# Gated linear attention and a maxout FFN: the first part in another order, the decay check ahead of the last stores

## The chip, the cores and the metric

The kernel runs on one core of one Trainium2 chip. A core has five engines that each follow a program of their own: PE multiplies matrices, DVE (VectorE), ACT (ScalarE) and POOL (GpSimd) work on elements, and SP issues transfers. ACT issues some transfers too. The engines wait for each other through semaphores, and each engine runs its instructions in the order of its program. The metric is the time of one execution on the device in microseconds. The kernel before takes 504.13 us, the median of 3 runs (503.74 to 504.51).

## What is computed

The first stage is a recurrence with a decay per feature, for 4 batches, 8 heads, 768 tokens and 48 features per head. The second is a feed-forward block on its output, whose hidden layer is the largest of three products:

```python
f = 1.0 / (1.0 + np.exp(-f_logit))
for t in range(S):
    state = f[:, :, t, :, None] * state + np.einsum('bhd,bhe->bhde', k[:, :, t], v[:, :, t])
    y[:, :, t] = np.einsum('bhd,bhde->bhe', q[:, :, t], state)
x = y.transpose(0, 2, 1, 3).reshape(B * S, H * D)         # 3072 tokens of 384
h = np.maximum(np.maximum(x @ w1, x @ w2), x @ w3)        # 384 to 768, three times
return (h @ w_out).astype(np.float32)                     # 768 to 384
```

q, k, v and f_logit are 32-bit floats. The weights come as 64-bit floats, and the kernel rounds them itself to 32 bits with integer operations on the two words of each number.

## The kernel before

**Units and groups.** The recurrence is done in chunks of 64 tokens. One unit is a chunk of two batches, so there are 24 units; unit u uses the v tile u mod 4 and the state u mod 2. Four units make a group of 512 tokens, and the FFN runs once per group, six times in all.

**One unit.** `sigmoids(u)` makes the gates, `after(u)` scans them backwards and makes kh, `before(u)` scans them forwards and makes qh, `carry(u)` decays the state. `keys(u)` turns kh for the state update. `pairs(u)` multiplies kh and qh within the chunk (L319) and masks the result into `at` (L322). `values(u)` multiplies `at` by v (L333) and adds up the new state (L342, L350). `finish(u)` adds the product of qh and the carried state (L363), and ACT copies the sums to `heads` (L369). The first eight units are loaded by tokens (L158) and turned by PE (L234). From unit 8 on, `load(u)` of an even unit loads two units in blocks of 32 tokens with 24 transfers (L173), all of them on SP, and DVE turns the blocks (L238). Part of the blocks' padding is set by POOL (`pad_blocks`, L143).

**Packing.** `pack` moves a stretch of `heads` to `xT`, the FFN's input, with ten transfers (L380) for a whole group, or ten for the first three units on SP and five on SP with five on ACT for the fourth.

**The FFN.** `ffn(g, xT)` is a generator of 22 steps. The first 18 are products of one block of one input matrix with xT (L392); each writes a PSUM tile `p`, of which there are two. ACT copies the first of three to `top` (L396), DVE takes the maxima (L398). The last four steps, i = 0 to 3, are the output products of one unit's tokens (L411). ACT copies each to a tile `o` (L414), of which the pool holds two, and SP stores `o` with two transfers (L418). `fill(n)` runs n steps at the place where it is called, so the calls of `fill` in the main loop decide how FFN steps and units alternate in every engine's program.

**Rounding.** The weights are loaded in 24 pieces to 12 `raw` tiles. `round_begin(n)` has two ACT instructions (L211, L216), two on DVE (L212, L213) and one on POOL (L217); `round_end(n)` is one more on DVE (L225). Pieces 0 to 2 are rounded before the first FFN, the others during it: each of its 18 steps ends with `round_end(r)` and `round_begin(r + 1)`.

**Order.** It is written out by hand under `manual_schedule`: each engine's instructions stand in the order in which the Python code emits them. The tiles' waits are added by the framework, and so are those of the transfers: eight semaphores are used in turn, and each transfer waits until the one before it on the same semaphore has landed, whichever engine issued that one.

**The end.** The result is right only if no chunk decays too far. After the last FFN step, DVE takes the least decay of all (`ends`), a 1x1 product on PE (L542) counts the violations, and every engine reads the count `low` (L732) and branches past a slow general version (L733).

Of the kernel before, what the change touches and what calls it, by code (L numbers as in the profile page):

```python
# [9 lines left out]
FP32 = mybir.dt.float32  # L10
I32 = mybir.dt.int32
U32 = mybir.dt.uint32
AF = mybir.ActivationFunctionType
ALU = mybir.AluOpType
# [40 lines left out]
def kernel(  # L55
# [32 lines left out]
    def fast():  # L88
        ctx = ExitStack()
        with ctx:  # L90
# [47 lines left out]
                    nc.vector.memset(t[:, :, D:DP], pad)  # L138

            def pad_blocks(i):  # L140
                for nm, pad in PADS.items():
                    for p0 in (32, 96):
                        nc.gpsimd.memset(blocks[nm][i][p0:p0 + 32, :, :, D - 32:], pad)  # L143

            NLD = 4
            BY_ROWS = 8
# [31 lines left out]
            def load_v(u):  # L178
                load_tokens(v_tiles[u % NLD], v, u)
# [20 lines left out]

            halfway = {}

            def round_begin(n):
                if n in raw:
                    words = raw[n].rearrange("p (c two) -> p c two", two=2)
                    lo, hi = words[:, :, 0], words[:, :, 1]

                    top = work.tile([128, PIECE], U32, name="top_bits", bufs=4)  # L210
                    nc.scalar.activation(top.bitcast(FP32), hi.bitcast(FP32), AF.Abs)  # L211
                    nc.vector.tensor_scalar(top.bitcast(FP32), top.bitcast(FP32), HI_MIN, None, op0=ALU.max)  # L212
                    nc.vector.tensor_scalar(top, top, 3, 0x3FFFFFF8, op0=ALU.logical_shift_left, op1=ALU.bitwise_and)  # L213

                    rest = work.tile([128, PIECE], U32, name="rest_bits", bufs=3)
                    nc.scalar.activation(rest, lo, AF.Copy, scale=2.0 ** -29)  # L216
                    nc.gpsimd.tensor_tensor(top, top, rest, op=ALU.add)  # L217
                    halfway[n] = (top, hi)

            def round_end(n):  # L220
                if n in raw:
                    top, hi = halfway.pop(n)
                    dst = pieces[n][0].bitcast(U32)
                    by = lambda t: t.rearrange("p (a c) -> p a c", a=dst.shape[1])
                    nc.vector.scalar_tensor_tensor(dst, by(hi), 0xC0000000, by(top),  # L225
                                                   op0=ALU.bitwise_and, op1=ALU.bitwise_or)
                    raw.pop(n)
# [157 lines left out]
            def ffn(g, xT):  # L385
                hm = work.tile([128, NJ, TOK], FP32, name="hm", bufs=1)
                for j in range(NJ):
                    top = None
                    for i in range(3):
                        p = ps_f.tile([128, TOK], FP32, name="p")  # L390
                        for kt in range(NK):
                            nc.tensor.matmul(p, lhsT=w_in[i][:, kt, j * 128:(j + 1) * 128], rhs=xT[:, kt, :],  # L392
                                             start=(kt == 0), stop=(kt == NK - 1))
                        if i == 0:
                            top = work.tile([128, TOK], FP32, name="top")
                            nc.scalar.copy(top, p)  # L396
                        else:
                            nc.vector.tensor_tensor(hm[:, j, :] if i == 2 else top, p, top, op=ALU.max)  # L398

                        if g == 0:  # L400
                            step, last = 3 * j + i, 3 * NJ
                            for r in range(*(3 + (len(pieces) - 3) * n // last for n in (step, step + 1))):
                                round_end(r)
                                if r + 1 < len(pieces):
                                    round_begin(r + 1)
                            load_weights(2, r + 1)
                        yield
                for i in range(GRP):
                    p = ps_f.tile([128, TOK], FP32, name="p")
                    for j in range(NJ):  # L410
                        nc.tensor.matmul(p[:, 0:DM], lhsT=hm[:, j, i * UT:(i + 1) * UT], rhs=w_out[:, j, :],  # L411
                                         start=(j == 0), stop=(j == NJ - 1))
                    o = work.tile([UT, DM], FP32, name="o")
                    nc.scalar.copy(o, p[:, 0:DM])  # L414
                    c, bp = divmod(g * GRP + i, 2)
                    for a in range(2):
                        t0 = (2 * bp + a) * S + c * C
                        nc.sync.dma_start(out=out[t0:t0 + C, :], in_=o[a * C:(a + 1) * C, :])  # L418
                    yield
# [3 lines left out]
            def fill(n):  # L423
                while n and pending:
                    try:
                        next(pending[0])
                        n -= 1
                    except StopIteration:
                        pending.pop(0)

            def new_xT():
                return work.tile([128, NK, TOK], FP32, name="xT")

# [3 lines left out]
            with tc.manual_schedule():  # L437
# [2 lines left out]
                load(1, one, "kq")  # L440
                load_v(0)
                load(2)
                load_v(1)
                load(3)
                load_weights(3)
                load_v(2)
                load_v(3)
                xT = new_xT()
                sigmoids(0)
# [8 lines left out]
                for u in range(2):  # L458
                    values(u)
                    keys(u + 1)  # L460
                    after(u + 2)
                    carry(u + 2)
                    pairs(u + 1)
                    finish(u)
                    before(u + 2)
                    if u == 0:
                        sigmoids(3)
                values(2)
                keys(3)
                finish(2)  # L470
                load_weights(3)
                load(GRP)
                load_v(GRP)
                round_begin(0)
                pairs(3)
                round_begin(1)
                round_begin(2)
                values(3)
                for n in range(3):
                    round_end(n)  # L480
                round_begin(3)

                nc.tensor.transpose(ps_tr.tile([128, 128], FP32, name="tr"), ident, ident)
                finish(3)
                pack(0, GRP - 1, xT, both)
                load_weights(3)
                load(GRP + 1)
                load_v(GRP + 1)
# [7 lines left out]
                fill(1)  # L496
                for u in range(GRP, NU):
                    n = u + 1
                    fill(2 if u % 2 and u > 2 * GRP else 1)
                    keys(u)  # L500
                    if u > GRP:
                        finish(u - 1)
                        if u % GRP == 3:
                            pack(0, 2, xT)
                        elif u % GRP == 0:
                            pack(3, 3, xT, both)
                    if u % GRP == 0:
                        if u > GRP:
                            pending.append(ffn(u // GRP - 1, xT))
                        xT = new_xT()  # L510
                    pairs(u)
                    if u + 2 < NU and (u % 2 == 0 or u + 2 < BY_ROWS):
                        load(u + 2)
                    if u + 2 < NU:
                        load_v(u + 2)
                    if n < NU:
                        sigmoids(n)
                    fill(1)
                    if n < NU:
                        after(n)  # L520
                    fill(1)
                    values(u)
                    if n < NU:
                        before(n)
                        carry(n)
                        if n in (5, 7):
                            pad_blocks(n // 2 % 2)
                    fill(1)
                    if u >= 2 * GRP:
                        fill(1)  # L530
                fill(1)
                finish(NU - 1)
                pack(3, 3, xT, both)
                pending.append(ffn(NU // GRP - 1, xT))
                fill(99)


            least = work.tile([128, 1], FP32, name="least")
            nc.vector.tensor_reduce(out=least, in_=ends.rearrange("p u a -> p (u a)"), op=ALU.min, axis=AX.X)
            nc.vector.tensor_scalar(least, least, P_MIN, None, op0=ALU.is_lt)  # L540
            n_low = ps_tr.tile([1, 1], FP32, name="tr")
            nc.tensor.matmul(n_low, lhsT=least, rhs=ones, start=True, stop=True)  # L542
            nc.vector.tensor_copy(low, n_low)

    def general():
        G, AHEAD = 128, 3
# [218 lines left out]
```

## Time and profile before

| | |
|---|---|
| median of 3 runs | 504.13 us |
| the profiled execution's own time | 504.31 us |
| its span, first to last instruction | 502.6 us |
| PE busy | 467.9 us (93%) |
| DVE busy | 217.2 us (43%) |
| ACT, POOL busy | 108.7 us, 98.7 us |
| mean granted clock of PE | 0.966 |
| first full FFN stretch begins | 46.34 us |
| last output product ends | 495.14 us |

The profile comes from one execution. Its page gives the busy time of each engine, the span in 40 slices, the transfers, the chain of waits that ended last, and groups of instructions. Further answers of the trace are a timeline (start and duration in us, engine, line, operation, output and inputs, and in brackets how long the engine had been idle and what ended that), busy time in chosen stretches, and sums of waits. PEld is PE's loading of weights, which overlaps its products. A matmul of 32-bit floats stands in the trace as two instructions. SPq and ACTq are the transfers issued by SP and ACT: the time given there is that of issuing, not of moving the data.

### The profile page before, as it was taken

What the parts mean: (1) busy time and instruction counts of PE and PEld (TensorE: products, weight loads), DVE (VectorE), ACT (ScalarE), POOL (GpSimd) and SP (SyncE); (2) the same over time, 40 slices, a digit from 0 to 9 for tenths busy, and PEclk for the clock granted to TensorE, in tenths of its full rate; (3) what the DMA queues carried; (4) which work ended last, traced back from release to release, by engine and by line L of the source; (5) the groups of instructions that cost most, each with busy time, mean ns of one, the idle gap of its engine ahead of it and who ended that gap; (6) DMA issues with size and microseconds to landing.
All of it is one profiled execution on the core that took longest, in us unless ns stands there. A gap on an engine that the chain in (4) does not pass through costs nothing.

```text
span 502.6 us, 9969 instructions
## 1 busy us (share of the span) xinstructions
PE 467.9 (93%) x4067; PEld 250.9 (50%) x4067; DVE 217.2 (43%) x346; ACT 108.7 (22%) x227; POOL 98.7 (20%) x132
## 2 busy tenths in 40 slices
PE   5755999996989999999999999999999999999994
PEld 4642555543635455645545654545644545544452
DVE  7852787787225435135535226533325620012100
ACT  2340445540212211202220211220220111100000
POOL 2111356564021212021112022112112200000000
PEclk9875999998999999999999999999999999999998
DMA  9995996720156612266602276402460011200011
GB/s 129 199 179 157 268 243 143 93 59 1 40 87 109 88 27 65 46 79 110 85 2 63 56 88 109 66 16 57 78 105 18 1 36 37 55 0 0 1 28 42
DMA packets 170007, 38.51 MB, mean 77 GB/s; under 512 B 154976, under 2 KB 168800, under 8 KB 169952
## 3 DMA queue, kind: packets, MB, share of 16 engines
q1 hardware_dynamic: 166208, 36.50, 41.5%
q10 hardware_dynamic: 3744, 1.28, 1.3%
q8 instruction: 34, 0.56, 0.5%
q14 instruction: 21, 0.17, 0.1%
HBM read 28.31 MB, written 4.72 MB: 66 GB/s over the span
## 4 chain that ended last, share of the span: by engine, by line
PE 80%; DVE 6%; DMA 4%; SPq 4%; ACT 1%; issue 1%; POOL 1%; ACTq 0%; DVEq 0%; POOLq 0%
PE p L392 53%; PE p L411 17%; SPq L158 3%; PE y L363 2%; PE y L333 2%; DMA xT<-heads 2%; PE a L319 2%; PE tr L306 2%; PE y L342 1%; DMA v_ld<-in_v_dram 1%; POOL top_bits L217 1%; PE tr L234 1%; DVE top_bits L213 1%; DMA k_ld<-in_k_dram 1%; DVE top_bits L212 1%
## 5 line engine op out<-in xcount | busy, mean ns | idle before, releaser
L392 PE MATMUL p<-xT,w_in 128*128 128x512 f32 x648 | 291.9, 602 | 7.3 <-DMA xT<-heads 5.1
L392 PEld LDWEIGHTS p<-xT,w_in 128*128 128x128 f32 x648 | 120.5, 191 | 147.0 <-issue 134.1
L411 PE MATMUL p<-w_out,hm 128*128 128x384 f32 x288 | 98.8, 501 | 4.3 <-DVE w_out L225 4.3
L411 PEld LDWEIGHTS p<-w_out,hm 128*128 128x128 f32 x288 | 55.5, 195 | 44.7 <-DVE w_out L225 5.6
L398 DVE TENSOR_TENSOR top<-p,top 128x512 f32<-128x512 f32 x36 | 24.8, 690 | 106.3 <-PE p L392 106.3
L396 ACT COPY top<-p 128x512 f32<-128x512 f32 x36 | 21.1, 586 | 191.5 <-PE p L392 191.5
L279 POOL COPY ends<-r 128x8 f32<-128x8 f32 x24 | 4.6, 193 | 194.2 <-DVE r L273 194.2
L398 DVE TENSOR_TENSOR hm<-p,top 128x512 f32<-128x512 f32 x36 | 24.6, 684 | 38.2 <-PE p L392 38.2
L322 DVE TENSOR_TENSOR at<-a,mask 128x512 f32<-128x512 f32 x24 | 16.5, 689 | 52.8 <-PE a L319 52.8
L217 POOL TENSOR_TENSOR top_bits<-top_bits,rest_bits 128x384 uint32<-128x384 uint32 x24 | 27.2, 1133 | 50.3 <-DVE top_bits L213 27.9
L414 ACT COPY o<-p 128x384 f32<-128x384 f32 x24 | 11.4, 477 | 107.8 <-PE p L411 99.0
L287 DVE TENSOR_TENSOR_SCAN prod<-gate,from_inv 128x520 f32<-128x520 f32 x24 | 32.4, 1349 | 0.0
L273 DVE TENSOR_TENSOR_SCAN r<-gate,from_one 128x520 f32<-128x520 f32 x24 | 30.9, 1288 | 2.9 <-issue 2.2
L369 ACT COPY heads<-y 64x256 f32<-64x256 f32 (+1 forms) x72 | 26.6, 369 | 14.3 <-PE y L363 13.3
L291 POOL TENSOR_TENSOR qh<-qt,prod 128x512 f32<-128x512 f32 x16 | 18.8, 1178 | 41.7 <-DVE qt L238 41.7
L333 PEld LDWEIGHTS y<-at,v_ld 64*64 64x64 f32 x768 | 13.9, 136 | 20.9 <-issue 16.7
L333 PE MATMUL y<-at,v_ld 64*64 64x64 f32 x768 | 17.3, 227 | 5.7 <-ACT rest_bits L216 2.7
L308 ACT COPY ks<-tr 128x512 f32<-128x512 f32 x22 | 12.9, 586 | 41.2 <-PE tr L306 40.9
L280 POOL TENSOR_TENSOR kh<-kt,r 128x512 f32<-128x512 f32 x16 | 19.0, 1186 | 14.2 <-DVE kt L238 14.2
L297 POOL TENSOR_TENSOR state<-st,ends 128x384 f32<-128x384 f32 x22 | 21.1, 958 | 0.2
L238 DVE STREAM_TRANSPOSE gate<-sig 128x512 f32<-128x512 f32 x16 | 11.3, 708 | 21.2 <-ACT sig L254 21.2
L319 PE MATMUL a<-qh,kh 48*64 48x64 f32 x768 | 16.5, 225 | 0.5 <-DVE qh L291 0.5
(64 smaller groups left out, 269.9 us busy)
## 6 DMA issues: line engine op xcount, KB each, us to landing
raw<-in_moe_w_dram SPq DMA_DIRECT2D x18, 384.0 KB, 5.1
v_ld<-in_v_dram SPq DMA_DIRECT2D x48, 96.0 KB, 3.3
out_dram<-o SPq DMA_DIRECT2D x48, 96.0 KB, 2.2
raw<-in_moe_w_out_dram SPq DMA_DIRECT2D x6, 384.0 KB, 4.1
xT<-heads SPq DMA_DIRECT2D x30, 72.0 KB, 2.1
f_ld<-in_f_logit_dram SPq DMA_DIRECT2D x32, 64.0 KB, 2.9
k_ld<-in_k_dram SPq DMA_DIRECT2D x32, 64.0 KB, 2.8
q_ld<-in_q_dram SPq DMA_DIRECT2D x32, 64.0 KB, 2.8
```

The lines of the kernel that those rows point to most:

```text
L217: nc.gpsimd.tensor_tensor(top, top, rest, op=ALU.add)
L273: nc.vector.tensor_tensor_scan(r[:, 0:LEN][:, ::-1], flat(gate)[:, ::-1], flat(from_one)[:, ::-1], 1.0, op0=ALU.mult, op1=ALU.max)
L280: (nc.vector if u < BY_ROWS else nc.gpsimd).tensor_tensor(kh.rearrange("p h a t -> p a h t"), kt, by_batch(r[:, 1:LEN + 1].rearrange("p (x ...
L287: nc.vector.tensor_tensor_scan(flat(prod), flat(gate_tiles[u % 2]), flat(from_inv[u % 2]), 1.0, op0=ALU.mult, op1=ALU.max)
L297: nc.gpsimd.tensor_tensor(t, states[u % 2], ends[:, u, :].unsqueeze(2).to_broadcast([128, 2 * HP, D]), op=ALU.mult)
L319: nc.tensor.matmul(p[t, par, hp * C:(hp + 1) * C], lhsT=kh[r, hp, a, :], rhs=qh[r, a, hp, :], start=True, stop=True)
L333: nc.tensor.matmul(y[o:o + DP, a, hp * C:(hp + 1) * C], lhsT=v_ld[s, 2 * hp + par, :], rhs=d["at"][s, par, hp, :], start=(hp == 0), stop=F ...
L369: nc.scalar.copy(heads[o, :, t0 + a * C:t0 + (a + 1) * C], y[i, a, 0:HP * C].rearrange("p (h t) -> p h t", h=HP))
L392: nc.tensor.matmul(p, lhsT=w_in[i][:, kt, j * 128:(j + 1) * 128], rhs=xT[:, kt, :], start=(kt == 0), stop=(kt == NK - 1))
L396: nc.scalar.copy(top, p)
L398: nc.vector.tensor_tensor(hm[:, j, :] if i == 2 else top, p, top, op=ALU.max)
L411: nc.tensor.matmul(p[:, 0:DM], lhsT=hm[:, j, i * UT:(i + 1) * UT], rhs=w_out[:, j, :], start=(j == 0), stop=(j == NJ - 1))
```

## The change

1. In the first part SP's transfers are in another order: f of unit 3 ahead of v of unit 1, v of unit 2 ahead of the first three weight pieces, and q and v of unit 4 behind the first pack.
2. `round_begin` is split. Its ACT part stays, with a fourth `rest_bits` tile, and the DVE and POOL part becomes `round_middle`. The first two pieces are begun ahead of `values(2)`; five pieces are begun before the first FFN instead of four, and within it `round_end(r)` is followed by the beginning of piece r + 2.
3. `busy(n)` emits n products of constants of 256 columns into a `p` tile that nobody reads: one after `pairs(1)`, `pairs(2)` and `pairs(3)`, and 14 after the first pack.
4. `pad_blocks` is a generator, and each step of the first FFN takes one of its POOL instructions.
5. At the start of unit 8 no FFN step is run, where one was; all later steps of the FFN move back by one place.
6. The check of the decay is emitted eight steps after the last FFN is appended, and no longer after the last step.

```diff
             def pad_blocks(i):
+
                 for nm, pad in PADS.items():
                     for p0 in (32, 96):
-                        nc.gpsimd.memset(blocks[nm][i][p0:p0 + 32, :, :, D - 32:], pad)
+                        yield nc.gpsimd.memset(blocks[nm][i][p0:p0 + 32, :, :, D - 32:], pad)
...
             def round_begin(n):
                 if n in raw:
...
                     top = work.tile([128, PIECE], U32, name="top_bits", bufs=4)
                     nc.scalar.activation(top.bitcast(FP32), hi.bitcast(FP32), AF.Abs)
+
+                    rest = work.tile([128, PIECE], U32, name="rest_bits", bufs=4)
+                    nc.scalar.activation(rest, lo, AF.Copy, scale=2.0 ** -29)
+                    halfway[n] = (top, rest)
+
+            def round_middle(n):
+                if n in raw:
+                    top, rest = halfway[n]
...
                     nc.vector.tensor_scalar(top.bitcast(FP32), top.bitcast(FP32), HI_MIN, None, op0=ALU.max)
                     nc.vector.tensor_scalar(top, top, 3, 0x3FFFFFF8, op0=ALU.logical_shift_left, op1=ALU.bitwise_and)
-                    rest = work.tile([128, PIECE], U32, name="rest_bits", bufs=3)
-                    nc.scalar.activation(rest, lo, AF.Copy, scale=2.0 ** -29)
                     nc.gpsimd.tensor_tensor(top, top, rest, op=ALU.add)
...
                                 round_end(r)
-                                if r + 1 < len(pieces):
-                                    round_begin(r + 1)
+                                if r + 2 < len(pieces):
+                                    round_begin(r + 2)
+                                    round_middle(r + 2)
                             load_weights(2, r + 1)
+                            next(pads, None)
                         yield
...
+                    if g == 0:
+                        next(pads, None)
                     o = work.tile([UT, DM], FP32, name="o")
...
+            def busy(n):
+
+                p = ps_f.tile([128, TOK], FP32, name="p")
+                for _ in range(n):
+                    nc.tensor.matmul(p[:, 0:256], lhsT=ident, rhs=from_one.rearrange("p x t -> p (x t)")[:, 0:256],
+                                     start=True, stop=True)
+
+            pads = iter(())
...
                 load(2)
+                load(3, one, "f")
                 load_v(1)
-                load(3)
+                load(3, one, "kq")
+                load_v(2)
                 load_weights(3)
-                load_v(2)
                 load_v(3)
...
                     pairs(u + 1)
+                    busy(1)
                     finish(u)
...
+                for n in range(2):
+                    round_begin(n)
                 values(2)
+                for n in range(2):
+                    round_middle(n)
                 keys(3)
                 finish(2)
                 load_weights(3)
-                load(GRP)
-                load_v(GRP)
-                round_begin(0)
+                load(GRP, one, "fk")
                 pairs(3)
-                round_begin(1)
+                busy(1)
                 round_begin(2)
+                round_middle(2)
                 values(3)
-                for n in range(3):
-                    round_end(n)
-                round_begin(3)
+                round_end(0)
...
                 finish(3)
+                round_end(1)
+                round_end(2)
                 pack(0, GRP - 1, xT, both)
+                for n in range(3, 5):
+                    round_begin(n)
+                    round_middle(n)
+                busy(14)
+                load(GRP, one, "q")
+                load_v(GRP)
                 load_weights(3)
...
-                    fill(2 if u % 2 and u > 2 * GRP else 1)
+                    fill(0 if u == 2 * GRP else 2 if u % 2 and u > 2 * GRP else 1)
                     keys(u)
...
                 pending.append(ffn(NU // GRP - 1, xT))
+                fill(8)
+
+                least = work.tile([128, 1], FP32, name="least")
+                nc.vector.tensor_reduce(out=least, in_=ends.rearrange("p u a -> p (u a)"), op=ALU.min, axis=AX.X)
+                nc.vector.tensor_scalar(least, least, P_MIN, None, op0=ALU.is_lt)
+                n_low = ps_tr.tile([1, 1], FP32, name="tr")
+                nc.tensor.matmul(n_low, lhsT=least, rhs=ones, start=True, stop=True)
+                nc.vector.tensor_copy(low, n_low)
                 fill(99)
-
-
-            least = work.tile([128, 1], FP32, name="least")
...
```

More of the change, by code (lines that the diff above doesn't have):

```diff
@@ L201, in fast, with words @@
             halfway = {}
+            def words(n):
+                w = raw[n].rearrange("p (c two) -> p c two", two=2)
+                return w[:, :, 0], w[:, :, 1]
             def round_begin(n):
                 if n in raw:
-                    words = raw[n].rearrange("p (c two) -> p c two", two=2)
-                    lo, hi = words[:, :, 0], words[:, :, 1]
+                    lo, hi = words(n)
                     top = work.tile([128, PIECE], U32, name="top_bits", bufs=4)
                     nc.scalar.activation(top.bitcast(FP32), hi.bitcast(FP32), AF.Abs)
+                    rest = work.tile([128, PIECE], U32, name="rest_bits", bufs=4)
[4 more added lines that the diff above has]
+                    top, rest = halfway[n]
                     nc.vector.tensor_scalar(top.bitcast(FP32), top.bitcast(FP32), HI_MIN, None, op0=ALU.max)
                     nc.vector.tensor_scalar(top, top, 3, 0x3FFFFFF8, op0=ALU.logical_shift_left, op1=ALU.bitwise_and)
-                    rest = work.tile([128, PIECE], U32, name="rest_bits", bufs=3)
-                    nc.scalar.activation(rest, lo, AF.Copy, scale=2.0 ** -29)
                     nc.gpsimd.tensor_tensor(top, top, rest, op=ALU.add)
-                    halfway[n] = (top, hi)
             def round_end(n):
                 if n in raw:
-                    top, hi = halfway.pop(n)
+                    (top, _), (_, hi) = halfway.pop(n), words(n)
                     dst = pieces[n][0].bitcast(U32)
@@ L526, in fast @@
                         if n in (5, 7):
-                            pad_blocks(n // 2 % 2)
+                            pads = pad_blocks(n // 2 % 2)
                     fill(1)
@@ L534, in fast @@
                 pending.append(ffn(NU // GRP - 1, xT))
-                fill(99)
-            least = work.tile([128, 1], FP32, name="least")
[L539 to L543, printed above, removed]
+                fill(8)
[5 more added lines that the diff above has]
+                nc.vector.tensor_copy(low, n_low)
+                fill(99)
     def general():
```

## The prediction

> **What bounds the kernel now.** I read the page's summary first, then busy time by stretch.
>
> ```profile
> PE 467.9 (93%) x4067; PEld 250.9 (50%) x4067; DVE 217.2 (43%) x346; ACT 108.7 (22%) x227; POOL 98.7 (20%) x132
> ...
> PEclk9875999998999999999999999999999999999998
> ```
> ```profile
> 40.00:46.30 6.30, 2.05 (x2) 0.50 (x2) 1.21 (x4) 0.36 (x1) 0.99 (x1) 0.50 0.54 126
> 46.30:52.40 6.10, 6.06 (x13) 3.45 (x14) 0.98 (x3) 2.27 (x5) 0.30 (x1) 0.50 1.13 258
> ...
> 80.00:105.00 25.00, 24.70 (x266) 13.12 (x268) 21.89 (x41) 10.71 (x22) 12.94 (x13) 1.00 0.66 104
> 116.20:121.50 5.30, 0.96 (x4) 0.33 (x3) 3.89 (x9) 0.00 (x0) 2.37 (x3) 0.93 0.00 0
> 121.50:127.50 6.00, 6.00 (x10) 3.23 (x11) 2.13 (x3) 0.48 (x1) 1.96 (x2) 0.50 0.00 0
> ```
>
> In each stretch: PE, PEld, DVE, ACT, POOL, granted clock, DMA. From about 142 to 495 us PE never stops; it loses time only before. While x is packed (40 to 46.3) it is nearly idle, then runs 6.1 us at half clock. From 80 to 105 DVE, which rounds the weights, is 88% busy. At 116 to 121.5 PE waits for it, and 6 us at half clock follow. So the front is worth some 20 us, and any new PE stall after 142 is paid in full.
>
> The waits and the timeline at the first group boundary show one more thing:
>
> ```profile
> PE p L392 <- ACT o L414: 2.2, 1, 2.2
> ```
> ```profile
> 140.87 0.48 ACT L414 COPY o<-p 128x384 f32<-128x384 f32 x1 [0.59 <-DMA out_dram<-o]
> ...
> 141.95 1.10 PE L392 MATMUL p<-xT,w_in 128*128 128x512 f32 x2 [2.18 <-ACT o L414]
> ```
>
> An output copy waited for an earlier store to free one of two o tiles, and PE waited for the copy, because there are two p tiles. At the later boundaries this is free. SP at the second of them:
>
> ```profile
> 206.84 8.01 PE L411 MATMUL p<-w_out,hm 128*128 128x384 f32 x24
> ...
> 210.24 3.10 SPq L380 DMA_DIRECT2D xT<-heads  x5
> ...
> 213.39 5.27 SPq L173 DMA_DIRECT2D f_ld<-in_f_logit_dram  x8
> ...
> 223.00 4.15 SPq L173 DMA_DIRECT2D q_ld<-in_q_dram  x8
> ...
> 228.78 3.32 SPq L418 DMA_DIRECT2D out_dram<-o  x4
> ```
>
> Between the pack and the next stores SP issues 24 loads and two v loads: 213.4 to 228.7. The stores behind them are late, but nobody wants their tiles for 18 FFN steps.
>
> [...] SP sat 24.09 us on four xT issues at 110.99. [...] matmuls restarted at 46.34 and 121.47 and each ran about 6.1 us at 0.50. [...] here PE's branch took 4318 ns.
>
> **The change, part by part**, against the profiled span of 502.6 us.
>
> *Transfers by need, first part.* values(2) waited for v(2), which landed at 27.66 behind three 384 KB weight pieces. Issued before them it lands near 22.9 (those pieces land 1.1 us apart, and the last q of unit 3 at 21.93). f(3) goes ahead of v(1): PE's 2.3 us wait at 17.7 for f(3) shrinks by the two issues passed, 1.3 us. The mask product at(2), ready at 25.45 before, then sets values(2), at about 24. ACT's roundings of pieces 0 and 1 (landing 24.0 and 25.1) go ahead of keys(3), at 0.54 us each, four in all, so ks(3) is ready near 26.6. DVE does four roundings (4 x 0.36) before at(3). finish(3) then ends near 31 instead of 39.15. The pack doesn't gain all 8: its issues wait for semaphores of f(4) and k(4), and the DMA engines were solid until 36.2 (landing of k(4)); the last xT lands 40.0 instead of 46.3. **FFN start: -6.3** (-3 to -7.5). Moving q(4) and v(4) behind the pack costs nothing: q(4) lands near 41, and its transpose comes 6 us after the start.
>
> *Products of constants.* 14 matmuls of 256 columns: half of the 0.86 us that one 128x512 product takes at full clock, so 0.43 each, 6.0 us in all, 12.0 at half clock. They begin near 31 and end near 37 to 39, inside the pack's wait. At full clock from the start, the FFN saves half of 6.1 us. But the last one ends 1 to 3 us before xT[...]. **-2** (0 to -3.1). The three single ones stand where PE waits for DVE or ACT: nothing; without cover, 0.43 to 0.86 each.
>
> *Roundings two ahead.* DVE's finishing instruction waited for POOL 7.4 + 1.2 us between 60 and 130, and 2.1 more behind POOL's pad memsets (3.5 us in a lump at 105.7, now one per step). That is 10.7 us back on DVE, against a lag of 5.4 us (PE done at 111.87, hm at 117.27) plus about 3 us because PE now runs the stage faster. Enough: PE's waits at 116.22 (2.86) and 119.99 (1.48) and the half of 6 us at half clock go. **-7** (-2 to -7.7).
>
> *Decay check.* SP's read of the flag (0.73, 0.19 and 0.04 with gaps, 496.88 to 498.00) moves ahead of the last eight stores; SP's branch comes 1.1 us earlier[...]. [...] **-0.9** (-0.3 to -1.2). The check's one matmul is 0.2 us.
>
> *No FFN step at the start of unit 8.* This small edit shifts every later step by one, through all four boundaries (units 8, 12, 16, 20). Before: output tiles i=0 and i=1, keys/finish/pack/pairs, 24 loads, i=2 and i=3. After: i=0, pack, loads, then i=1, i=2, i=3. In SP's program two stores now stand ahead of the pack and six behind the loads. There are two o tiles: the copy of i=3 must wait for the store of i=1, and the second FFN step for that copy's p tile. With times from the start of i=0, taken from the later boundaries: i=0 to 3.9 (L411, 7.74 for two), keys to pairs 1.6, i=1 and i=2 to 13.4, values(12) 1.1, i=3 to 18.4, FFN step one (2.57) to 21.0; there PE stops. SP: the pack ends 5.2 after keys begin (352.67 to 357.88), at 9.1; from the first load to the second landed store 19.0, 18.5 and 18.3 in the three trace boundaries, so 27.6; the copy is done (0.48) at 28.2. PE idles 7.2 to 8.1, take 7.5. [...] **10.1 each, +30.3** for three (+26 to +36).
>
> Unit 8 is worse. In the order of the program the second to sixth DMA of the pack of units 4 to 6 now each wait for a DMA of ACT's own pack, which comes only after finish(7). Before, the ninth and tenth waited so (that was the 24.09 us). ACT's first xT lands 4.8 after keys begin (129.09 to 133.88), at 8.7; then nine xT (0.62 each), v(9) 1.4, the i=0 store 1.2 (to 16.9), the pack 3.1, loads 13.9, v(10) 1.5, the i=1 store 1.2 plus 2.2 to land: 38.8, copied at 39.5. xT is complete only at 22. PE idles 18.4 to 22, and 24.7 to 39.6: 18.6; with a clock loss of 2.6, and less the 2.6 of PE waits there before (138.2 to 141.95). **+18.7** (+12 to +22).
>
> Sum: 502.6 - 6.3 - 2 - 7 - 0.9 + 30.3 + 18.7 = 535.4. The profiled execution took 504.31 by the clock outside, the median is 504.13, so 1.5 lies around the span: **537 us**.
>
> **Rivals.** *A, as summed* (0.60): 530 to 544. *B, the front gives half* (0.20): if POOL or ACT stays late, PE still stalls at w_out[...]: 8 us less gain, 545. DVE's 88% speaks for it, the 10.7 us of waits against. *C, unit 8 is no worse than the others* (0.14): if the pack's semaphore order binds less than the program shows, that boundary costs 10.1 less 2.6 and not 18.7: 526. *D, the stores land in time* (0.05), the faster side: the loads between are 13.9 us of SP; under 6.4 us of them (21.0 less the pack's end 9.1, v 1.5, store 1.3, landing 2.2 and copy 0.5) PE would find its p tile free. Then 504.1 - 16.2 - 2.6 = 485. Against it: three boundaries of the trace have 13.8 to 15.3. That the edits cancel to nothing has 0.01.
>
> Faster or slower means by more than 0.2%, about what a measurement of this kernel can tell from no change: faster 0.05, same 0.01, slower 0.94. 80% range 524 to 548: all of A, most of B and C; D lies outside.
>
> **What would show it.** In the profile after: PE at L401 waiting for ACT's copy at L427 about 7 to 8 us three times and some 15 us once, ACT at L427 waiting for DMA out; half clock after each; out stores on SP after each 24 loads; FFN start near 40 at clock 1.00; no wait of L422 for w_out. Wrong if PE runs through the boundaries, or if the front gains under 8 us.

## The result, and the profile after

The changed kernel takes 535.54 us (median of four, 534.21 to 536.72) against 504.00 (503.74 to 504.51): 1.062 times as long, with a 95% interval of 1.060 to 1.065. The profiled execution took 535.54, its span 533.7. The forecast was 537 with a range of 524 to 548.

The page's summary and chain come first. Lines moved in the file by one to thirteen: L401 is the FFN product (L392 before), L422 the output product (L411), L427 the copy to `o` (L414), L431 the store of `o` (L418), L174 the later loads (L173).

```profile
PE 477.8 (90%) x4101; PEld 256.3 (48%) x4101; DVE 224.1 (42%) x346; ACT 109.0 (20%) x227; POOL 99.3 (19%) x132
...
PEclk9979999999599999889999969999979999999999
...
PE 68%; SPq 14%; DVE 7%; DMA 5%; issue 3%; ACT 1%; POOL 1%; ACTq 0%; DVEq 0%; POOLq 0%
PE p L401 49%; PE p L422 10%; SPq L174 9%; SPq L159 3%; PE y L372 2%; PE y L342 2%; DMA out_dram<-o 2%; SPq L389 2%; PE p L448 1%; PE a L328 1%; PE tr L315 1%; PE y L351 1%; DVE prod L296 1%; DMA raw<-in_moe_w_out_dram 1%; DMA v_ld<-in_v_dram 1%
```

PE now does 90% of a longer span. The clock keeps one early dip, in the third slice (half clock from 29.6 to 36.4 us). It has lost those from 40 us on, and has four new ones, one at each group boundary. SP's loads (`SPq L174`) hold 9% of the chain that sets the end.

The same stretches as before the change, in the view of busy time by stretch (PE, PEld, DVE, ACT, POOL, granted clock, DMA share, GB/s):

```profile
40.00:46.30 6.30, 6.30 (x25) 3.73 (x24) 2.65 (x6) 2.23 (x5) 2.04 (x3) 1.00 0.81 209
46.30:52.40 6.10, 6.10 (x19) 2.87 (x18) 5.93 (x10) 1.77 (x4) 2.50 (x4) 1.00 1.39 188
80.00:105.00 25.00, 25.00 (x320) 13.92 (x319) 23.73 (x41) 10.95 (x24) 13.88 (x16) 1.00 0.49 66
116.20:121.50 5.30, 5.30 (x78) 3.26 (x77) 2.03 (x5) 0.15 (x1) 1.37 (x2) 1.00 0.38 94
```

The first part does what it should. From 40 us PE is full and at full clock (up to 41 with the products of constants), DVE is 95% busy from 80 to 105 with PE never short of weights, and the idle 116 to 121.5 is gone. What comes after takes it back. The waits (us in total, times, longest) and the timeline, first at unit 8 and then at unit 12:

```profile
ACT o L427 <- DMA out_dram<-o: 67.6, 5, 18.3
...
PE p L401 <- ACT o L427: 36.7, 4, 15.3
...
SPq L389 <- DMA xT<-heads: 16.1, 1, 16.1
...
PE tr L574 <- DVE least L572: 1.3, 1, 1.3
```
```profile
112.70 6.29 SPq L389 DMA_DIRECT2D xT<-heads  x10
...
120.58 1.94 SPq L431 DMA_DIRECT2D out_dram<-o  x2
122.62 3.10 SPq L389 DMA_DIRECT2D xT<-heads  x5
125.76 4.31 SPq L174 DMA_DIRECT2D f_ld<-in_f_logit_dram  x8
...
134.36 4.20 SPq L174 DMA_DIRECT2D q_ld<-in_q_dram  x8
138.60 1.39 SPq L159 DMA_DIRECT2D v_ld<-in_v_dram  x2
140.09 4.54 SPq L431 DMA_DIRECT2D out_dram<-o  x6
...
143.02 0.48 ACT L427 COPY o<-p 128x384 f32<-128x384 f32 x1 [18.31 <-DMA out_dram<-o]
...
143.56 2.93 PE L401 MATMUL p<-xT,w_in 128*128 128x512 f32 x3 [15.30 <-ACT o L427]
...
227.08 1.22 PE L401 MATMUL p<-xT,w_in 128*128 128x512 f32 x1 [6.82 <-ACT o L427]
```

One pair of stores stands ahead of the last five transfers of the pack, and three pairs stand behind 24 loads. The copy of output tile 3 needs the tile that the store of tile 1 still holds, and so waits until 143.02. PE waits for that copy, 15.30 us here, 6.82 at unit 12, 7.20 and 7.40 at units 16 and 20.

### The profile page after: what moved, and what is told of

Its sections match the earlier page's. It is cut to its first block, busy times and chain, and to the rows that moved or that the text cites. A ratio compares the mean times of both kernels' runs of the same rounds, so it can differ in the third digit from the quotient of the medians.

```text
span 533.7 us, 10055 instructions
## 1 busy us (share of the span) xinstructions
PE 477.8 (90%) x4101; PEld 256.3 (48%) x4101; DVE 224.1 (42%) x346; ACT 109.0 (20%) x227; POOL 99.3 (19%) x132
## 4 chain that ended last, share of the span: by engine, by line
PE 68%; SPq 14%; DVE 7%; DMA 5%; issue 3%; ACT 1%; POOL 1%; ACTq 0%; DVEq 0%; POOLq 0%
PE p L401 49%; PE p L422 10%; SPq L174 9%; SPq L159 3%; PE y L372 2%; PE y L342 2%; DMA out_dram<-o 2%; SPq L389 2%; PE p L448 1%; PE a L328 1%; PE tr L315 1%; PE y L351 1%; DVE prod L296 1%; DMA raw<-in_moe_w_out_dram 1%; DMA v_ld<-in_v_dram 1%
## 5 line engine op out<-in xcount | busy, mean ns | idle before, releaser
L401 PE MATMUL p<-xT,w_in 128*128 128x512 f32 x648 | 298.7, 613 | 37.1 <-ACT o L427 36.7
L401 PEld LDWEIGHTS p<-xT,w_in 128*128 128x128 f32 x648 | 123.2, 196 | 182.3 <-issue 135.2
L422 PE MATMUL p<-w_out,hm 128*128 128x384 f32 x288 | 96.6, 490 | 0.5 <-DVE w_out L234 0.5
L407 DVE TENSOR_TENSOR top<-p,top 128x512 f32<-128x512 f32 x36 | 24.7, 687 | 165.5 <-PE p L401 165.3
L422 PEld LDWEIGHTS p<-w_out,hm 128*128 128x128 f32 x288 | 53.8, 190 | 38.1 <-issue 2.4
L427 ACT COPY o<-p 128x384 f32<-128x384 f32 x24 | 11.5, 477 | 151.0 <-PE p L422 80.1
L296 DVE TENSOR_TENSOR_SCAN prod<-gate,from_inv 128x520 f32<-128x520 f32 x24 | 35.0, 1459 | 0.0
L342 PEld LDWEIGHTS y<-at,v_ld 64*64 64x64 f32 x768 | 14.2, 137 | 16.8 <-issue 14.5
```

The lines of the kernel that those rows point to most:

```text
L296: nc.vector.tensor_tensor_scan(flat(prod), flat(gate_tiles[u % 2]), flat(from_inv[u % 2]), 1.0, op0=ALU.mult, op1=ALU.max)
L342: nc.tensor.matmul(y[o:o + DP, a, hp * C:(hp + 1) * C], lhsT=v_ld[s, 2 * hp + par, :], rhs=d["at"][s, par, hp, :], start=(hp == 0), stop=F ...
```

## The experiments

**Theory.** The one FFN step left out at the start of unit 8 makes all four stalls, through two `o` tiles and SP's order of issue, and the rest of the change is a gain. **Rivals:** the stalls come from the new first part, which leaves the queues later; the stores are late because transfers are slow or semaphores hold them, whatever the queue; PE would have waited at those places anyway.

A time below is the median of all executions. A ratio and its interval are of means that leave out the profiled execution, against the kernel before on the same chip: 504.26 us beside the first four versions, 503.81 beside the four that undo one part, 502.72 beside the other four. So a ratio is not just the quotient of two medians.

### The step put back, and the step alone

```diff
-fill(0 if u == 2 * GRP else 2 if u % 2 and u > 2 * GRP else 1)
+fill(2 if u % 2 and u > 2 * GRP else 1)
```

> The changed kernel with the FFN step at the start of unit 8 put back, all else kept. Theory (the shift of the steps by one makes all four stalls): the 36.7 us that PE waits for ACT's output copy go, and of the 19.1 us at half clock after the restarts (5.5, 3.9, 6.1, 3.6) half, 9.6; the small wait that the kernel before has at its first boundary (2 to 3) comes back: 535.5 - 36.7 - 9.6 + 2 = 491, range 486 to 494, below the kernel before by 10 to 18. Rival (the stalls come from the order of the first part, which leaves the queues later by the first boundary): the waits stay, 525 or more. Rival (PE would have waited there for something else anyway): 498 to 510.

Measured: 493.16 us (492.91 to 494.04), 0.9785 of before (0.9767 to 0.9803). The reverse edit in the kernel before:

```diff
-fill(2 if u % 2 and u > 2 * GRP else 1)
+fill(0 if u == 2 * GRP else 2 if u % 2 and u > 2 * GRP else 1)
```

> The kernel before with only the FFN step at the start of unit 8 left out. Theory: four stalls, three of 7.1 and one of about 15 us, and 9.6 for the clock, less the 2.6 that it waited there: 504 + 43 = 547, range 543 to 553. The prediction's own sum would give 504 + 49 = 553. Rival (the shift costs only with the new first part): 504 to 510.

Measured: 548.24 us (546.78 to 549.77), 1.0877 of before (1.0843 to 1.091). Its waits:

```profile
ACT o L414 <- DMA out_dram<-o: 64.9, 5, 19.0
...
PE p L392 <- ACT o L414: 34.8, 4, 14.2
```

Four waits, the longest 14.2 us, as in the changed kernel, with the old first part. The step costs 42.4 us on the new first part (535.54 - 493.16) and 44.0 on the old one (548.24 - 504.26). The first rival is out. With the step put back, one wait of another kind is left at unit 8:

```profile
PE p L401 <- DMA xT<-heads: 5.7, 1, 5.7
```

In the old order of steps PE has no output tiles left to do while `xT` of the second group is packed. The kernel before waited 2.2 us for an output copy at this place. So the third rival holds for 5.7 of the 36.7 us, and at one boundary alone.

### Three o tiles, and the stores on another queue

Both keep the step left out. The first has one more `o` tile, and three tiles instead of four for the scaled low words, to make room:

```diff
-o = work.tile([UT, DM], FP32, name="o")
+o = work.tile([UT, DM], FP32, name="o", bufs=3)
-rest = work.tile([128, PIECE], U32, name="rest_bits", bufs=4)
+rest = work.tile([128, PIECE], U32, name="rest_bits", bufs=3)
```

> The changed kernel, its shift kept, with three o tiles instead of two (and three tiles for the scaled low words instead of four, to make room). Theory (the copy of output tile 3 waits only because there are two o tiles and the store of tile 1 stands behind the loads): that copy now waits for the store of tile 0, issued ahead of the loads, so all four stalls go: 486 to 494 as with the step put back. Rival (the transfers themselves are too slow at the boundaries, or xT is late there): a stall of 3 to 7 us stays at each, 505 to 520.

Measured: 488.10 us (487.41 to 493.03), 0.9719 of before (0.9666 to 0.9773). Its page and timeline at unit 8:

```profile
PE 465.4 (96%) x4101; PEld 250.9 (52%) x4101; DVE 223.8 (46%) x346; ACT 109.5 (23%) x227; POOL 99.2 (20%) x132
...
PEclk9999999998999999999999999999999999999998
```
```profile
117.94 1.22 SPq L431 DMA_DIRECT2D out_dram<-o  x2
...
122.99 4.30 SPq L174 DMA_DIRECT2D f_ld<-in_f_logit_dram  x8
...
138.05 4.04 SPq L431 DMA_DIRECT2D out_dram<-o  x6
```

The six stores are as late as before, 20 us after the first two, and PE waits for none of them: tile 3 takes the `o` of tile 0, whose store went ahead of the loads. All four waits are gone. The 5.7 us for `xT` that the old order has at unit 8 are absent too, since the shifted order gives PE three output tiles to do meanwhile. The second leaves two `o` tiles and moves the stores to ACT's queue:

```diff
-nc.sync.dma_start(out=out[t0:t0 + C, :], in_=o[a * C:(a + 1) * C, :])
+nc.scalar.dma_start(out=out[t0:t0 + C, :], in_=o[a * C:(a + 1) * C, :])
```

> The changed kernel, its shift and its two o tiles kept, with all output stores issued from ACT's queue instead of SP's. Theory (the stores are late because they stand behind 24 loads in SP's program): they land 3 to 4 us after their copy, the three later stalls go; ACT pays about 1.2 us a pair of stores, which is 48 pairs x 1.2 less what is hidden, and ACT is idle three quarters of the time: 486 to 500. Rival (the stores are late because the DMA engines are full with the loads, or because their semaphores wait for loads): waits of 5 us or more stay at the boundaries, 515 to 540.

Measured: 492.23 us (491.45 to 493.81), 0.9763 of before (0.9744 to 0.9783). The timeline of ACT at unit 12:

```profile
199.76 1.16 ACTq L431 DMA_DIRECT2D out_dram<-o  x2
200.97 0.48 ACT L427 COPY o<-p 128x384 f32<-128x384 f32 x1 [1.23 <-PE p L422]
201.48 1.12 ACTq L431 DMA_DIRECT2D out_dram<-o  x2
205.30 0.48 ACT L427 COPY o<-p 128x384 f32<-128x384 f32 x1 [3.85 <-PE p L422]
```

The same stores beside the same loads land in time, and the third copy waits for PE alone. So the DMA engines were not too slow: the place in SP's program was it, and the second rival is out at the later boundaries. At unit 8 PE still waited 2.7 us, for `xT`.

### A smaller dose, and the shift one group later

The eight `q` loads of a pair of units go behind the stores of tiles 1 and 2 (step left out, two `o` tiles):

```diff
-load(u + 2)
+load(u + 2, one, "fk")
...
+if u + 2 < NU and (u % 2 == 0 or u + 2 < BY_ROWS):
+    load(u + 2, one, "q")
 values(u)
```

> The changed kernel (shift, two o tiles) with the eight q loads of each later pair of units issued behind the stores of output tiles 1 and 2 instead of ahead of them. Theory (what PE waits for is the time that SP spends on the loads ahead of the store): eight issues take 4.15 us, so the three later waits of 7.1 shrink to about 3.0 and leave no half clock behind, and the one at unit 8 of 15.3 to 11.1: 535.5 - 3 x (4.15 + 2.3) - 4.15 = 512, range 508 to 517. Rival (the store waits for the loads' semaphores or for busy DMA engines): 525 or more.

Measured: 516.81 us (514.79 to 518.44), 1.0278 of before (1.0245 to 1.031). The timeline of SP and PE at unit 12, then two stretches there:

```profile
208.49 4.15 SPq L174 DMA_DIRECT2D k_ld<-in_k_dram  x8
212.74 1.44 SPq L159 DMA_DIRECT2D v_ld<-in_v_dram  x2
214.27 2.51 SPq L431 DMA_DIRECT2D out_dram<-o  x4
216.87 4.30 SPq L174 DMA_DIRECT2D q_ld<-in_q_dram  x8
...
217.81 2.14 PE L401 MATMUL p<-xT,w_in 128*128 128x512 f32 x3 [2.66 <-ACT o L427]
```
```profile
215.20:218.60 3.40, 0.79 (x2) 0.49 (x3) 0.00 (x0) 0.97 (x2) 0.00 (x0) 1.00 0.72 155
218.60:222.00 3.40, 3.40 (x5) 1.35 (x4) 0.00 (x0) 0.00 (x0) 0.00 (x0) 0.51 0.69 87
```

Taking 4.15 us of issues away shortens the three later waits from 6.82, 7.20 and 7.40 to 2.66, 3.17 and 2.88: by 4.2 on average. That is the price of queue time one for one. (At unit 8 the wait fell further, from 15.30 to 8.73; why is open.) My total was 5 too low, because I had let the half clock go with waits so short. At unit 12 it stayed for 3.4 us (0.51 in the second stretch above), which is 1.7 lost; three times that is 5.1, an estimate from this one boundary. The further fall at unit 8 is offset in part in this trace by a first FFN product that comes 1.0 us later (42.01).

The last of this group leaves out the step at unit 12 instead of unit 8:

```diff
-fill(0 if u == 2 * GRP else 2 if u % 2 and u > 2 * GRP else 1)
+fill(0 if u == 3 * GRP else 2 if u % 2 and u > 2 * GRP else 1)
```

> The changed kernel (two o tiles) with the FFN step left out at the start of unit 12 instead of unit 8: unit 8 keeps the old order of steps, the three later boundaries the new one. Theory (each of the three costs 7.1 us of waiting and 2.3 of clock, by the trace of the changed kernel): 493.2 + 28.3 = 521, range 518 to 524. If each costs 10.1, as the prediction had it: 523.5. Rival (the later stalls follow from the late state in which unit 8 leaves the queues): they shrink or go, under 510.

Measured: 527.09 us (525.51 to 527.84), 1.0469 of before (1.0443 to 1.0495): 6 us above the theory's number and 4 above the prediction's. The waits of SP in the stretch around unit 12, and PE's timeline there:

```profile
SPq L431 <- DMA xT<-heads: 8.7, 1, 8.7
```
```profile
219.16 6.14 PE L401 MATMUL p<-xT,w_in 128*128 128x512 f32 x9 [10.58 <-ACT o L427]
```

The first store of tile 0, at the head of SP's queue, had got the turn of a semaphore of an `xT` transfer from ACT and waited for it, some 4 us past the copy that it stores. Pack, loads and the later stores all came some 4 us later, and PE waited 10.58 us where the changed kernel waits 6.82. Which transfer waits for which is dealt out by eight semaphores in turn, so moving one step can change the deal at the next boundary. (The trace of the changed kernel shows it: 470 transfers on eight semaphores, and in all 462 pairs of neighbours on one semaphore the second was issued after the first had landed.) The three later boundaries cost 25.8 us of waiting in this trace. They do so without a stall for an output copy at unit 8, so the later stalls don't follow from that one: this experiment's own rival is out. Unit 8, in the old order, has a wait of 5.4 us for `xT`.

### The parts of the first part, one at a time

All four are edits to the version with three `o` tiles (488.10 above, and once more below), undoing one part. Without the cover:

```diff
-busy(14)
```

> The version with the shift and three o tiles (488.1, 485.6 in the span), without the 14 products of constants between the pack and the first FFN product. The prediction priced them at 2 us (0 to 3.1). Theory (they keep PE's clock up while xT is awaited): PE is idle for about 6 us before the first FFN product, runs the first 6 us at half clock, and the time rises by 2 to 3 to 490 to 491. Rival (the half clock in which they themselves run, or their ending at the moment at which xT lands, makes them worth nothing): 487 to 489.

Measured: 490.70 us (488.85 to 491.43), 0.9723 of before (0.9701 to 0.9745). The roundings begun one piece ahead:

```diff
-if r + 2 < len(pieces):
-    round_begin(r + 2)
-    round_middle(r + 2)
+if r + 1 < len(pieces):
+    round_begin(r + 1)
+    round_middle(r + 1)
...
-for n in range(3, 5):
+for n in range(3, 4):
```

> The same version, with the roundings begun one piece ahead as before instead of two (the second pass and the pad memsets one per step stay). The prediction gave the roundings two ahead and the pads 7 us (2 to 7.7). Theory (beginning two ahead is what takes DVE's waits for POOL away): DVE ends the rounding some 5 us later, PE waits for w_out at the first output products and runs at half clock after it: 493 to 495. Rival (the earlier start of pieces 0 to 4 and the spread memsets do most of it): 488 to 490.

Measured: 493.45 us (491.78 to 494.94), 0.9784 of before (0.976 to 0.9808). The decay check behind the last output tile:

```diff
 fill(8)
-least = work.tile([128, 1], FP32, name="least")
...
-nc.vector.tensor_copy(low, n_low)
 fill(99)
+least = work.tile([128, 1], FP32, name="least")
...
+nc.vector.tensor_copy(low, n_low)
```

> The same version with the decay check back behind the last output tile. The prediction gave the move 0.9 us (0.3 to 1.2); the traces have 7.37 us from the last output copy to the end before, 6.25 after: 1.1. But PE waits 1.3 us for the check's compare in the new place, ahead of the last output products. Theory (both count, and cancel): 487.5 to 488.5. Rival (only the tail counts): 489.2.

Measured: 489.57 us (487.25 to 489.62), 0.9699 of before (0.9676 to 0.9721). The transfers in the old order:

```diff
-load(3, one, "f")
 load_v(1)
-load(3, one, "kq")
-load_v(2)
+load(3)
 load_weights(3)
+load_v(2)
...
-load(GRP, one, "fk")
+load(GRP)
+load_v(GRP)
...
-load(GRP, one, "q")
-load_v(GRP)
```

> The same version with the order of transfers of the kernel before: f of unit 3 with its k and q and after v of unit 1, v of unit 2 behind three weight pieces, q and v of unit 4 ahead of the pack. The prediction gave the transfers by need 6.3 us (3 to 7.5), together with ACT's early roundings, which stay here. Theory: the mask product and values of unit 2 wait for v of unit 2 until about 27.7 instead of 24.5, the pack comes 3 us later, and q(4) and v(4) ahead of it cost 4 issues of 0.6: 492 to 495. Rival (the DMA engines are full until xT anyway, so that the order within decides little): 488 to 490.

Measured: 493.04 us (490.09 to 494.91), 0.9764 of before (0.9732 to 0.9795). And the base again, on the same chip as the last version:

> The version with the shift and three o tiles once more, as a base on the same chip: 486 to 490.

Measured: 490.61 us (487.55 to 491.80), 0.9751 of before (0.9726 to 0.9776), just above what was expected. Two measurements of one kernel, 0.9719 and 0.9751, are the yardstick for the four, since none was measured on their own chip: a part undone has to cost more than about 2 us to be seen. One piece ahead comes out highest (0.9784, 1.7 to 3.3 us above), though its interval still meets that of the base; the trace below speaks for it. The old transfers (0.9764) are at the edge. The cover and the place of the check show nothing. The expectations were written for a base of 488.1: by their numbers the cover, one piece ahead and the old transfers came out as the theory had them, and the check nearer its rival. With the base at 490.61 that is no proof.

The four come to some 5 us at most, while the whole is 12.5 to 14 (504 times 0.0249 to 0.0281). The rest may lie in what was not undone (the earlier start of the roundings, the spread memsets, the shift with its third `o` tile), or in parts that cover for each other. How the whole divides is left open.

The traces say more than the times. One piece ahead, the stretch from the first output product to the second group's first FFN product is 24.7 us (105.35 to 130.08), against 21.5 in the second measurement of the base (101.96 to 123.45); PE waits for `w_out` again:

```profile
PE p L422 <- DVE w_out L234: 2.1, 2, 1.5
...
PE a L328 <- POOL qh L300: 1.6, 1, 1.6
```

Without the cover, the first FFN product waits and then runs at half clock until 45.7 (granted clock 0.50 from 36 to 42 us, 0.69 from 42 to 48):

```profile
39.56 2.04 PE L401 MATMUL p<-xT,w_in 128*128 128x512 f32 x2 [4.43 <-DMA xT<-heads]
```

With the old transfers the first FFN product starts at 45.86, against 38.2 to 42.3 with the new ones and the cover. With the check behind the last output tile, it is 7.5 us from the start of the last output copy to the end, against 6.3 in the base, and PE's wait of 1.30 us for the compare is gone: in the traces the two cancel.

### The check's compare ahead of its product

```diff
-fill(8)
+fill(4)
 nc.vector.tensor_reduce(out=least, in_=ends.rearrange("p u a -> p (u a)"), op=ALU.min, axis=AX.X)
 nc.vector.tensor_scalar(least, least, P_MIN, None, op0=ALU.is_lt)
+fill(4)
 n_low = ps_tr.tile([1, 1], FP32, name="tr")
```

> The version with the shift and three o tiles, with DVE's two instructions of the decay check four FFN steps ahead of its product on PE. Theory: PE's wait of 1.3 us for that compare goes, 1.0 to 1.3 us below the same version without it. Rival (DVE then delays a maximum that PE waits for, or it is hidden): within 0.5.

Measured: 487.44 us (486.33 to 489.53), 0.9701 of before (0.9677 to 0.9724), 3.2 us below the base on the same chip. PE's wait of 1.30 us is gone in the trace. The rest of the 3.2 lies in the scatter of the base described below: of the base's six executions four have a lower mean clock (0.987 to 0.990), of these six only one (0.986). The median is the lowest of the case, but the ratio can't be told from the 0.9699 of the version with the check behind the last output tile.

## Why the prediction was right, point by point

The sum, term by term, in the profiled executions:

| Term | Predicted | Measured | From |
|---|---|---|---|
| start of the FFN | -6.3 | -5.3 | 46.34 to 41.00 |
| clock at that start | -2 | -3.05 | half of 6.1, now at 1.00 |
| roundings | -7 | -6.3 | remainder of 16.85, below |
| unit 8 | +18.7 | +16.1 | 15.30 + 0.25 + 2.75 - 2.18 |
| units 12, 16, 20 | +30.3 | +28.2 | 21.4 idle, 6.8 clock |
| decay check | -0.9 | +0.2 | tail -1.1, wait +1.3 |
| sum | +32.8 | +29.8 | spans differ by 31.1 |

The first FFN product of the second group started at 141.95 before and at 125.10 after, 16.85 earlier. Of these, 2.18 are the small wait that the prediction had booked under unit 8; taking the first two rows off as well leaves 6.3 for the roundings, which is a remainder and not a measurement. Some 1.3 us of the span are in no row. The total came out closer than its parts: rows that made it too high by 5.8 us together (the clock, unit 8, units 12 to 20) stand against 4.1 us that made it too low or are in no row. The mechanism at the boundaries was right; that the sum ends within 2 us is in part luck.

*Transfers.* values(2) began at 24.54 (24 said). But finish(3) ended near 33.3 and not 31, and `xT` landed at 40.87 and not 40.0. PE ran at half clock from 29.6 to 36.4, which no step of the sum had. Where that did not happen, the FFN started at 38.2 to 39.0.

*Products of constants.* They ran from 33.3 to 41.16, the first 3.1 us at half clock, right up to the landing of `xT` at 40.87. So the gap of 1 to 3 us never came, and the FFN started at full clock (1.00 from 40 to 46.3). But they can run too long. With the check behind the last tile and with the shift at unit 12, both with the half clock near 30 us, `xT` was complete at 41.09 and 41.20 and the FFN started at 41.84 and 42.29, as the last of them ended. What they are worth in time the runs can't tell.

*Roundings.* DVE is 95% busy from 80 to 105 and PE's waits for `w_out` fell to 0.5 us, where none was forecast. Rival B is out. What does it is shown in part: beginning two ahead, taken back alone, costs some 1.7 to 3.3 us of the 6 to 7, so the earlier start or the spread memsets may do the rest; these were not tried apart.

*Units 12, 16, 20.* 7.1 us of waiting each (7.5 said) and 2.3 of clock (2.6 said, which was my estimate): the copy, the store of tile 1 and the 24 loads are the mechanism, shown by three `o` tiles, by the other queue and by the smaller dose. Rival D is out.

*Unit 8.* The longer queue is there as described: SP sat 16.1 us before the pack until ACT's first `xT` transfer had landed (112.63), and the store of tile 0, copied by 109.14, was issued at 120.58. The copy of tile 3 was done 39.8 us after the first output product (39.5 said). PE waited 15.30 us for the copy (15 said), but 0.25 and not 3.6 for `xT`: PE itself needed 21.2 us from the first output product to its FFN step, where the sum had 18.4. Two short waits account for 2.0 of the difference (0.55 for `w_out`, 1.42 for qh). Rival C, unit 8 no worse than the others, is out.

*Decay check.* This step failed, a forecast gain of 0.9 us that was none. SP's earlier branch gave its 1.1 us in the tail. But the check's product on PE now stands in the middle of the last FFN and waits 1.30 us for DVE's compare. The prediction had priced that product at 0.2 us, and not asked what it waits for.

## What to carry to other kernels

A change that leaves one step out moves every later step against every queue. Write down, for each tile that is used again, which store must have left and what stands ahead of that store in its issuing queue: here eight loads of 0.52 us each cost PE 4.2 us, one for one. If the store has to stay where it is, one more buffer or another queue takes the wait away; here each turned 6% slower into 2 to 3% faster, the rest of the change included.

When a small check is moved into a busy stretch, its operands have to be ready there: issue its first half some steps ahead.

## What the runs showed of the hardware that I had not expected

The expectation for the later `q` loads had waits of about 3 us leave no half clock behind. The traces show it after shorter ones. With the later `q` loads PE waited 2.66 us at unit 12, was busy for 0.79 of the 3.40 us up to 218.6, and then ran 3.4 us at 0.51, as shown above. In the first measurement of three `o` tiles it waited 1.42 us for qh, was busy for 1.98 of 3.40 us, and again 3.4 us at 0.51 followed:

```profile
106.30:109.70 3.40, 1.98 (x68) 1.56 (x67) 1.26 (x3) 1.86 (x5) 2.43 (x3) 1.00 0.05 12
109.70:113.10 3.40, 3.40 (x7) 1.69 (x6) 1.00 (x3) 0.63 (x1) 0.57 (x2) 0.51 0.30 80
```

The same wait stands in four more traces with no half clock behind it: 1.42 us in the changed kernel, 1.4 with the check behind the last output tile and in the second measurement of three `o` tiles (granted clock 1.00 from 105 to 125 us in all three), and 1.4 with the stores on ACT's queue (PEclk 9 in the slices from 98 to 123 us). What decides is open.

The front varies in the same way. Of ten traces with the new transfers and the cover, six show half clock near 30 us (6.8 us from 29.6 in the changed kernel), and three show none (1.00 from 30 to 42 us). The FFN starts at 41.0 to 42.3 in five of the six, and at 38.2 to 39.0 in the three. The tenth, with the later `q` loads, starts it at 42.01; its clock there is not shown. The executions of the version with three `o` tiles fall into two sets in the same way, by the mean clock that is on record for each: five of 487.4 to 488.4 us have 0.992 to 0.998, five of 490.5 to 493.0 have 0.982 to 0.990. By my estimate, 6.8 us at half clock in 486 take off 0.007. So the clock goes with the two sets; that it was lost near 30 us in the slower five is argued and not shown, since none of them has a trace.

After the long waits the clock came back 3.6 to 6.1 us after PE restarted, not after a fixed time: in the changed kernel the half-clock stretches themselves last 17.1, 6.8, 10.2 and 6.8 us at units 8, 12, 16 and 20.
